# A gated linear attention and two dense layers on one core: the carried state is applied head by head on quarters of the array

## The chip, the core and the metric

The kernel runs on one core of a Trainium2 chip. TensorE (PE) multiplies matrices into PSUM; VectorE (DVE), ScalarE (ACT) and GpSimd (POOL) work element by element; DMA queues move data. The metric is the device time of one execution in microseconds (us); smaller is better. Nothing but float32 values enters or leaves.

## What is computed

For 4 batches of 8 heads, 768 steps and head size 48, each head keeps a 48x48 state that is decayed row by row with a gate and gets an outer product added at each step. The outputs of all heads are rows of 384 values, 3072 in all, which then pass through two dense layers with different activations.

```
f = 1 / (1 + exp(-f_logit))
for t in range(S):
    state = f[:, :, t, :, None] * state + einsum('bhd,bhe->bhde', k[:, :, t], v[:, :, t])
    y[:, :, t] = einsum('bhd,bhde->bhe', q[:, :, t], state)
h = max(x @ w_in, 0);  x = (h * h) @ w_out           # first layer, 384 -> 2048 -> 384
h = x @ w_in2;  g = h if h > 0 else exp(min(h, 0)) - 1;  out = g @ w_out2
```

## The kernel before

The 768 steps of each batch are cut into chunks of 128, so there are 24 chunks, numbered in order of time with the four batches taken in turn: chunk g belongs to batch g % 4. Two heads form a pair; there are four pairs, and their 2 x 48 channels lie on rows 0 to 47 and 64 to 111 (`HD`). A chunk passes through these steps:

- `a_gate`, `a_decay`: the gate, and its running products (two scans on VectorE).
- `a_scale`: queries and keys are multiplied with the products, on VectorE and GpSimd.
- `a_carry`: VectorE multiplies the batch's carried state with the decay of the chunk (line 186), and ScalarE copies it into `diag`, which holds a block-diagonal 112x112 matrix for each pair (line 188, two copies; the rest of `diag` was set to zero at the start).
- `a_scores`: keys are transposed (`tp`), and keys times queries make the scores of each head (`sc`, line 172), two heads at a time on the upper and the lower rows of the array. `a_mask` copies the scores under a mask into `ss`.
- `a_state`: keys times values (`kv`, line 201), which VectorE adds to the carried state in the same step (line 203).
- `a_out`: the outputs. For each pair and head, values times masked scores (line 229: 8 matmuls of all 128 rows, the two heads of a pair on the left and the right columns); then for each pair one matmul of `diag` with the queries on the whole array (line 234: 4 matmuls). ScalarE copies the results from PSUM into `x1` (lines 239 and 244), and six small DMAs distribute the fourth pair's rows.
- `a_hi`, `a_lo`: the outputs are split into a rounded part and a rest for the dense layers.

The first four chunks have no carried state and go by `a_direct`. The other 20 (chunks 4 to 23) have the matmuls of `diag`.

The dense layers work on six blocks of 512 rows each, and each block on 16 slices of 128 hidden features, so a layer has 96 units. A unit is `up` (9 matmuls into `ph`, line 343), `between` and `low` (the activation, on ScalarE, VectorE and GpSimd) and `down` (9 matmuls into `y`, line 395). Each of these 18 matmuls streams 512 columns. `down` runs two units behind `up`.

The order of the work is written out by hand: a plan gives each unit number ("slot") the steps that are issued ahead of that slot's `up`. Chunks 4 to 7 are finished during the first block (slots 0 to 15), and four further chunks during each of the next four blocks. During the first block the weights of the first layer are made as well, one slice per slot: a 64-bit word is decoded into float32 by ScalarE (line 46) and three VectorE instructions (lines 48, 51, 52), and is then split by ScalarE (`w`, line 312) and VectorE (`w`, line 313) into a rounded part and a rest. Unit f needs both. Each engine works strictly through its own list; within a slot the list has the chunk's steps first, then the load, decoding and splitting of weights.

Of the kernel before, what the change touches and what calls it, by code (L numbers as in the profile page):

```python
# [11 lines left out]
F32 = mybir.dt.float32  # L12
# [4 lines left out]
AF = mybir.ActivationFunctionType  # L17
ALU = mybir.AluOpType
PSUM = bass.MemoryType.PSUM

B, H, S, D = 4, 8, 768, 48
NT, DM, DFF = B * S, H * D, 2048
NG = NT // 128
NC = NG // B
NF = DFF // 128
NK = DM // 128
NP = H // 2
# [9 lines left out]
FIRST = (0, 3, 6, 8), (-6, -2, 2, 6)  # L37
STAGED = 15
DMIN = 2.0**-52


def decode(nc, raw, out):
# [12 lines left out]
def chunked(ctx, tc, ff, qk, vk, vz, wraw, mask, ident, flag, out):  # L55
# [23 lines left out]
    ds = [one.tile([ROWS, 2, 521], F32, name=f"ds{i}") for i in range(2)]  # L79
    ss = [one.tile([128, 2, NP, 128], F32, name=f"ss{i}") for i in range(2)]  # L80
    state = [one.tile([ROWS, NP, 48], F32, name=f"state{b}") for b in range(B)]
    diag = one.tile([ROWS, NP, ROWS], F32, name="diag")
    dlast = [one.tile([ROWS, NP], F32, name=f"dlast{b}") for b in range(B)]
    x2d = dram.tile([NK, 128, NT], F32, name="x2d")
    wst = dram.tile([NF, 128, 2, 2, DM], F32, name="wst")
# [97 lines left out]
    def a_carry(g):  # L183

        now = state[g % B]
        V.tensor_tensor(out=now, in0=now, in1=st[g]["wc"].unsqueeze(2).to_broadcast([ROWS, NP, 48]), op=ALU.mult)
        for lo, hi in HD:
            A.activation(diag[lo:hi, :, lo:hi], now[lo:hi], AF.Copy)

    def a_state(g):  # L190
        s = st[g]
        now = state[g % B]
        if g < NG - B:
            kvp = ps_a.tile([128, NP, 48], F32, tag="a", name=f"kv{g}")
            for p in range(NP):
                for j, (lo, hi) in enumerate(((0, 64), (64, ROWS))):
                    if g >= B:
                        v = s["vk"][:, p, j]
                    else:
                        v = s["vz"][:, p, j, 0:48] if p < NK else s["vz"][:, :, j, 96:112]  # L200
                    PE.matmul(kvp[lo:hi, p], s["kt"][:, p, lo:hi], v, start=True, stop=True)  # L201
            if g >= B:
                V.tensor_tensor(out=now, in0=kvp[:ROWS], in1=now, op=ALU.add)
            else:
                A.activation(now, kvp[:ROWS], AF.Copy)

    def a_direct(g):
        s = st[g]
        yp = ps_a.tile([128, NK, 128], F32, tag="a", name=f"yp{g}")
        for k in range(NK):  # L210
            for p, c in ((k, 0), (NK, 48)):
                for j in range(2):
                    PE.matmul(
                        yp[64 * j:64 * j + 64, k], s["vz"][:, k, j, c:c + 64], ss[g % 2][:, j, p],
                        start=c == 0, stop=c > 0,
                    )
        s["yp"] = yp

    def a_out(g):
        s = st[g]  # L220
        q = s["qk"][:, 0].rearrange("r (p t) -> r p t", p=NP)
        y3p = ps_a.tile([128, 128], F32, tag="a", name=f"y3p{g}")
        yp = ps_a.tile([128, NK, 128], F32, tag="a", name=f"yp{g}")

        outs = [(p, yp[:, p] if p < NK else y3p) for p in (NK, 0, 1, 2)]
        for p, o in outs:
            v = s["vk"][:, p].rearrange("r j d -> r (j d)")
            for j, c in enumerate((slice(0, 64), slice(48, 96))):
                PE.matmul(  # L229
                    o[64 * j:64 * j + c.stop - c.start], v[:, c], ss[g % 2][:, j, p],  # L230
                    start=p in (0, NK), stop=False, skip_group_check=True,
                )
        for p, o in outs:
            PE.matmul(o[:ROWS], diag[:, p], q[:, p], start=False, stop=p >= NK - 1, skip_group_check=True)  # L234
        x1 = two.tile([128, NK + 1, 128], F32, tag="x1", name=f"x1_{g}")
        y3, x1 = x1[:ROWS, NK], x1[:, :NK]

        for lo, hi in HD:
            A.activation(y3[lo:hi], y3p[lo:hi], AF.Copy)
        for k in range(NK):  # L240
            for lo, _ in HD:
                nc.sync.dma_start(out=x1[lo + 48:lo + 64, k], in_=y3[lo + 16 * k:lo + 16 * k + 16])
        for lo, hi in HD:
            A.activation(x1[lo:hi], yp[lo:hi], AF.Copy)
        s["x1"] = x1

    where = {}
# [168 lines left out]


    prepare = (a_gate,), (a_decay,), (a_scale, a_carry)
    finish = (a_scores, a_transposed, a_mask), (a_state, a_out), (), (), (a_hi, a_lo)
    for g in range(B, NG):  # L420
        i, o = where[g]
        d = o // 128
# [24 lines left out]
    with tc.manual_schedule():  # L447
        V.memset(lim, DMIN)
        V.memset(mn, 1.0)
        V.memset(ss[0], 0.0)  # L450
        G.memset(ss[1], 0.0)
        G.memset(diag, 0.0)

        warm = ps_a.tile([128, 512], F32, tag="a", name="warm")
        for _ in range(3):
            PE.matmul(warm, ss[0][:, 0, 0], ss[0][:, 0].rearrange("r p t -> r (p t)"), start=True, stop=True)
        steps = {
            "I": lambda: nc.sync.dma_start(out=idt, in_=ident),
            "M": lambda: nc.sync.dma_start(out=msk, in_=mask),
            "f": load_f, "q": load_qk, "v": load_v, "r": lambda f: load_raw(0, f),  # L460
            "g": a_gate, "d": a_decay, "c": a_scale, "s": a_scores, "t": a_transposed, "m": a_mask, "k": a_state,
            "y": a_direct, "h": a_hi, "l": a_lo,
            "w": lambda f: decode_weights(0, f), "W": lambda f: split_weights(0, f),
            "U": lambda f: up(0, f), "B": lambda f: between(0, f),
            "L": lambda f: low(0, f),
        }
        for o in START.split():
            steps[o[0]](*(int(c) for c in o[1:]))
        for u in range(2, len(units) + 2):

            last = units[u - 2] == (n1 - 1, NF - 1)
            todo = plan.get(u, ())
            for f, args in () if last else todo:
                f(*args)
            if u < len(units):
                up(*units[u])
            down(*units[u - 2])
            for f, args in todo if last else ():
                f(*args)
            if u < len(units):  # L480
                between(*units[u])
                low(*units[u])


def general(ctx, tc, nat, wraw, ident, out):
# [45 lines left out]
    with tc.For_i(0, 2, 1) as h, tc.For_i(0, B, 1) as b:  # L531
        y = yd[bass.ds(2 * b + h, 1)].rearrange("n p e j t -> (n p) e j t")
        for k in range(NK):
            for j in range(2):
                nc.sync.dma_start(out=x[64 * j:64 * j + 48, k], in_=y[k, :, j])
                nc.sync.dma_start(out=x[64 * j + 48:64 * j + 64, k], in_=y[NP - 1, 16 * k:16 * k + 16, j])
        for layer in range(2):
            V.memset(acc, 0.0)
            with tc.For_i(0, NF, 1) as ff:
# [43 lines left out]
def _layout(q, k, v, f_logit, moe_w_in, moe_w_out, moe2_w_in, moe2_w_out):  # L583
    fwd = np.arange(128)
    outward = np.r_[fwd[:64][::-1], fwd[64:]]

    def heads(a, order, pad):
        a = a.reshape(B, NP, 2, NC, 128, D)[:, :, :, :, order]
        t = np.full((NC, B, 2, 64, NP, 128), pad, a.dtype)
        t[:, :, :, :D] = a.transpose(3, 0, 2, 5, 1, 4)  # L590
        return t.reshape(NG, 128, 512)[:, :ROWS]


    ff = np.full((NG, ROWS, 521), -64.0, np.float32)
    ff[:, :, :520].reshape(NG, ROWS, 2 * NP, 65)[:, :, :, 1:] = heads(f_logit, outward, 8.0).reshape(NG, ROWS, 2 * NP, 64)
    qk = np.stack([heads(q, fwd, 0.0), heads(k, outward, 0.0)], axis=2)
    vk = v.reshape(B, NP, 2, NC, 128, D)[:, :, :, :, outward].transpose(3, 0, 4, 1, 2, 5).reshape(NG, 128, DM)
    vz = np.zeros((B, 128, NK, 2, 112), v.dtype)
    vp = vk[:B].reshape(B, 128, NP, 2, D)
    vz[..., :48] = vp[:, :, :NK]  # L600
    vz[..., 96:] = vp[:, :, NK].reshape(B, 128, 2, NK, 16).transpose(0, 1, 3, 2, 4)
    vz = vz.reshape(B, 128, -1)
    rows = []
    for kk in range(NK):
        for j in range(2):
            rows += [(2 * kk + j) * D + e for e in range(48)]
            rows += [(6 + j) * D + 16 * kk + e for e in range(16)]
    rows = np.array(rows)

    def weights(w_in, w_out):  # L610
        a = w_in.reshape(NK, 128, NF, 128).transpose(2, 1, 0, 3).reshape(NF, 128, DM)
        return np.concatenate([a, w_out.reshape(NF, 128, DM)], axis=2)

    wraw = np.stack([weights(moe_w_in[rows], moe_w_out), weights(moe2_w_in, moe2_w_out)]).view(np.int64)
    nat = np.zeros((B, NP, 4, 2, 64, S), np.float32)
    for c, a in enumerate((f_logit, q, k, v)):
        nat[:, :, c, :, :D] = a.reshape(B, NP, 2, S, D).transpose(0, 1, 2, 4, 3)
    nat = nat.reshape(B, NP, 4, 128, S)[:, :, :, :ROWS]
    mask = (outward[:, None] <= fwd[None, :]).astype(np.int32)
    return {  # L620
        "ff": ff, "qk": qk, "vk": vk, "vz": vz, "nat": nat, "wraw": wraw, "mask": mask,
        "ident": np.eye(128, dtype=np.float32),
    }
# [13 lines left out]
```

## Time and profile before

| | |
|---|---|
| median of 3 runs | 944.69 us (943.04 to 944.89) |
| profiled execution, its own time | 943.66 us |
| its span, first to last instruction | 941.9 us |
| mean granted TensorE clock | 0.981 of full speed |
| busy: TensorE matmuls / VectorE / ScalarE / GpSimd | 913.2 / 564.4 / 455.8 / 327.1 us |

The rows further down are from this one execution. A float32 matmul of an attention step leaves two records in the trace, one for each part of its weights; a matmul of the dense layers leaves one. Records of a row marked xN follow each other or overlap: the row's first number is the start of its first record, the second the time from there to the end of its last. A record's end is modelled and lies past the start of the next, so the pace of a stream is read from starts. A number in brackets is the idle time of the engine ahead of the row, with what ended it.

### The profile page before, as it was taken

What the parts mean: (1) busy time and instruction counts of PE and PEld (TensorE: products, weight loads), DVE (VectorE), ACT (ScalarE), POOL (GpSimd) and SP (SyncE); (2) the same over time, 40 slices, a digit from 0 to 9 for tenths busy, and PEclk for the clock granted to TensorE, in tenths of its full rate; (3) what the DMA queues carried; (4) which work ended last, traced back from release to release, by engine and by line L of the source; (5) the groups of instructions that cost most, each with busy time, mean ns of one, the idle gap of its engine ahead of it and who ended that gap; (6) DMA issues with size and microseconds to landing.
All of it is one profiled execution on the core that took longest, in us unless ns stands there. A gap on an engine that the chain in (4) does not pass through costs nothing.

```text
span 941.9 us, 13099 instructions
## 1 busy us (share of the span) xinstructions
PE 913.2 (97%) x4841; PEld 740.8 (79%) x4841; DVE 564.4 (60%) x834; ACT 455.8 (48%) x791; POOL 327.1 (35%) x295
## 2 busy tenths in 40 slices
PE   6888989999999999999999999999999999999996
PEld 4766768888888888788888888888888888888885
DVE  8888886667667766775401166456555555555543
ACT  4457664554445445454444444444444444443543
POOL 5222323443444443444233232332332333233231
PEclk8799899999999999999999999999999999999998
DMA  8445423444433443442246530100100100100001
GB/s 277 141 141 192 131 67 123 135 137 141 141 108 109 143 142 126 154 146 78 94 158 213 174 135 1 57 12 1 56 12 1 56 13 0 57 12 1 34 0 37
DMA packets 30791, 88.44 MB, mean 94 GB/s; under 512 B 4992, under 2 KB 9728, under 8 KB 30720
## 3 DMA queue, kind: packets, MB, share of 16 engines
q1 hardware_dynamic: 28848, 77.32, 24.7%
q10 hardware_dynamic: 1872, 10.22, 3.2%
q8 instruction: 39, 0.64, 0.3%
q14 instruction: 32, 0.26, 0.1%
HBM read 64.52 MB, written 22.02 MB: 92 GB/s over the span
## 4 chain that ended last, share of the span: by engine, by line
PE 87%; DVE 8%; issue 2%; ACT 1%; DMA 1%; POOL 0%; ACTq 0%; DVEq 0%
PE y L395 40%; PE ph L343 40%; PE sc L172 2%; DVE dec L51 1%; DVE w L313 1%; PE yp L229 1%; PE yp L234 1%; DVE ds L136 1%; DVE dec L52 1%; PE kv L201 1%; DVE dec L48 1%; PE y3p L234 1%; DVE ss L181 1%; PE tp L166 1%; PE y3p L229 1%
## 5 line engine op out<-in xcount | busy, mean ns | idle before, releaser
L382 POOL TENSOR_TENSOR gl<-gg,gh 128x512 fp32r<-128x512 f32 x175 | 232.5, 1328 | 489.6 <-PE ph L343 193.5
L395 PE MATMUL y<-gh,w 128*128 128x512 f32 x576 | 179.9, 393 | 0.0
L395 PE MATMUL y<-gh,wf 128*128 128x512 f32 (+1 forms) x582 | 179.6, 390 | 0.0
L343 PE MATMUL ph<-xh,w 128*128 128x512 f32 x576 | 158.6, 410 | 11.2 <-ACT w L312 7.5
L368 DVE SCALAR_TENSOR_TENSOR t<-r,t 128x512 f32<-128x512 f32 (+1 forms) x97 | 71.5, 737 | 162.4 <-ACT r L367 161.3
L343 PE MATMUL ph<-xh,wf 128*128 128x512 f32 (+1 forms) x582 | 147.8, 389 | 0.0
L364 ACT ACTIVATE r<-ph 128x512 f32<-128x512 f32 (+1 forms) x97 | 57.6, 594 | 186.0 <-PE ph L343 176.7
L343 PEld LDWEIGHTS ph<-xh,w 128*128 128x128 f32 x576 | 107.1, 192 | 38.5 <-ACT w L312 9.2
L395 PEld LDWEIGHTS y<-gh,w 128*128 128x128 f32 x576 | 108.9, 189 | 24.9
L395 PEld LDWEIGHTS y<-gh,wf 128*128 128x128 f32 x582 | 108.9, 188 | 24.4 <-ACT gh L371 0.2
L343 PEld LDWEIGHTS ph<-xh,wf 128*128 128x128 f32 x582 | 108.6, 188 | 23.7
L395 PE MATMUL y<-gl,wf 128*128 128x512 f32 (+1 forms) x291 | 112.8, 388 | 0.0
L395 PE MATMUL y<-gl,w 128*128 128x512 f32 x288 | 112.5, 391 | 0.0
L356 ACT ACTIVATE r<-ph 128x512 f32<-128x512 f32 x96 | 56.9, 593 | 91.1 <-PE ph L343 73.5
L343 PE MATMUL ph<-xl,w 128*128 128x512 f32 x288 | 84.7, 403 | 0.2 <-DVE xl L269 0.2
L343 PE MATMUL ph<-xl,wf 128*128 128x512 f32 (+1 forms) x291 | 82.2, 391 | 0.0
L362 DVE TENSOR_TENSOR gh<-r 128x512 fp32r<-128x512 f32 x64 | 44.5, 696 | 48.6 <-ACT r L356 48.1
L369 DVE SCALAR_TENSOR_TENSOR gg<-ph,t 128x512 f32<-128x512 f32 (+1 forms) x97 | 66.6, 686 | 10.0
L343 PEld LDWEIGHTS ph<-xl,w 128*128 128x128 f32 x288 | 56.1, 195 | 13.2 <-DVE xl L269 0.6
L357 ACT ACTIVATE gg<-r 128x512 f32<-128x512 f32 x96 | 60.8, 633 | 8.0 <-ACT r L356 0.4
L395 PEld LDWEIGHTS y<-gl,wf 128*128 128x128 f32 x291 | 54.7, 188 | 12.1 <-DVE gl L376 0.2
L395 PEld LDWEIGHTS y<-gl,w 128*128 128x128 f32 x288 | 54.2, 188 | 12.4
(84 smaller groups left out, 1067.3 us busy)
## 6 DMA issues: line engine op xcount, KB each, us to landing
raw<-wraw SPq DMA_DIRECT2D x19, 768.0 KB, 4.5
wst<-w SPq DMA_DIRECT2D x16, 768.0 KB, 4.0
wf<-wst SPq DMA_DIRECT2D x16, 768.0 KB, 4.3
qk<-qk SPq DMA_DIRECT2D x24, 448.0 KB, 5.4
raw<-wraw ACTq DMA_DIRECT2D x13, 768.0 KB, 4.4
ff<-ff SPq DMA_DIRECT2D x22, 227.9 KB, 4.5
x2d<-yo SPq DMA_DIRECT2D x18, 256.0 KB, 2.3
x<-x2d SPq DMA_DIRECT2D x18, 256.0 KB, 3.1
```

Source lines behind the costliest of these rows:

```text
L172: PE.matmul(sc[j][:, p], k[lo:hi, p], q[lo:hi, p], start=True, stop=True)
L229: PE.matmul(o[64 * j:64 * j + c.stop - c.start], v[:, c], ss[g % 2][:, j, p], start=p in (0, NK), stop=False, skip_group_check=True,)
L234: PE.matmul(o[:ROWS], diag[:, p], q[:, p], start=False, stop=p >= NK - 1, skip_group_check=True)
L343: PE.matmul(ph, w[:, a, 0, 128 * k:128 * k + 128], b[:, k, c], start=(m == 0), stop=(m == len(todo) - 1))
L356: A.activation(r[:, c], ph, AF.Relu)
L357: A.activation(gg[:, c], r[:, c], AF.Square)
L362: V.tensor_tensor(out=gh[:, c], in0=r[:, c], in1=r[:, c], op=ALU.mult)
L364: A.activation(r[:, c], ph, AF.Relu, scale=-1.0)
L368: V.scalar_tensor_tensor(out=t[:, c], in0=r[:, c], scalar=1.0, in1=t[:, c], op0=ALU.add, op1=ALU.mult)
L369: V.scalar_tensor_tensor(out=gg[:, c], in0=ph, scalar=0.0, in1=t[:, c], op0=ALU.max, op1=ALU.add)
L382: G.tensor_tensor(out=gl, in0=gg, in1=gh, op=ALU.subtract)
L395: PE.matmul(yp_[i][m][:, c], w[:, a, 1, 128 * m:128 * m + 128], b[:, c], start=(f == 0 and n_ == 0), stop=(f == NF - 1 and n_ == 2 and c.s ...
```

## The change

The block-diagonal matrices are gone, with their two ScalarE copies per chunk and their clearing at the start. In `a_out` the carried state of each head is now the weight of a matmul of its own, 48 rows by 48 columns, with the same head's rows of the queries: 8 matmuls in place of 4. The input rows of a head (0 or 64) are fixed; its output rows are 0 or 64, and for pairs 2 and 3 the two heads are swapped (`at_`), so that four heads of two pairs use the four quarters of the array. Pairs 0 and 1 go to one PSUM tile, pairs 2 and 3 to another; four copies of 48x256 take them to `x1` in place of two of 48x128 and two of 48x384, the fourth pair's tile first. The values' matmuls (8, all 128 rows) are now all 48 columns wide. Because the state is read by `a_out` now, the addition of `kv` to it becomes a step of its own, `a_add`, one slot later. The host's tables are permuted in the same manner (the values of the first four chunks, the rows of the first weight matrix).

```
+def at_(p, j):
+    return j if p < 2 else 1 - j
...
-        for lo, hi in HD:
-            A.activation(diag[lo:hi, :, lo:hi], now[lo:hi], AF.Copy)
...
-                V.tensor_tensor(out=now, in0=kvp[:ROWS], in1=now, op=ALU.add)
+                s["kv"] = kvp
...
+    def a_add(g):
+        if g < NG - B:
+            now = state[g % B]
+            V.tensor_tensor(out=now, in0=st[g]["kv"][:ROWS], in1=now, op=ALU.add)
...
-        y3p = ps_a.tile([128, 128], F32, tag="a", name=f"y3p{g}")
-        yp = ps_a.tile([128, NK, 128], F32, tag="a", name=f"yp{g}")
-        outs = [(p, yp[:, p] if p < NK else y3p) for p in (NK, 0, 1, 2)]
-        for p, o in outs:
-            v = s["vk"][:, p].rearrange("r j d -> r (j d)")
-            for j, c in enumerate((slice(0, 64), slice(48, 96))):
+        o = [ps_a.tile([128, 2, 128], F32, tag="a", name=f"o{g}_{i}") for i in range(2)]
+        for p in (0, 2, 1, 3):
+            for j in range(2):
+                r = 64 * at_(p, j)
                 PE.matmul(
-                    o[64 * j:64 * j + c.stop - c.start], v[:, c], ss[g % 2][:, j, p],
-                    start=p in (0, NK), stop=False, skip_group_check=True,
+                    o[p // 2][r:r + 48, p % 2], s["vk"][:, p, j], ss[g % 2][:, j, p],
+                    start=p % 2 == 0, stop=False, skip_group_check=True,
                 )
-        for p, o in outs:
-            PE.matmul(o[:ROWS], diag[:, p], q[:, p], start=False, stop=p >= NK - 1, skip_group_check=True)
+        for p in (0, 2, 1, 3):
+            for j, (lo, hi) in enumerate(HD):
+                r = 64 * at_(p, j)
+                PE.matmul(
+                    o[p // 2][r:r + 48, p % 2], state[g % B][lo:hi, p], q[lo:hi, p],
+                    start=False, stop=p % 2 == 1, skip_group_check=True,
+                )
...
-        for lo, hi in HD:
-            A.activation(y3[lo:hi], y3p[lo:hi], AF.Copy)
-        for lo, hi in HD:
-            A.activation(x1[lo:hi], yp[lo:hi], AF.Copy)
+        for i in (1, 0):
+            for lo, hi in HD:
+                A.activation(x1[lo:hi, 2 * i:2 * i + 2], o[i][lo:hi], AF.Copy)
...
-    finish = (a_scores, a_transposed, a_mask), (a_state, a_out), (), (), (a_hi, a_lo)
+    finish = (a_scores, a_transposed, a_mask), (a_state, a_out), (a_add,), (), (a_hi, a_lo)
...
-        G.memset(diag, 0.0)
```

On TensorE, the outputs of chunk 8 stand like this before; `y3p8` and `yp8` are the PSUM tiles of the fourth and of the first three pairs, `vk8` the values, `qk8` the queries.

```order
L229 MATMUL y3p8_1288<-ss0_89,vk8_1066 64x128
L229 MATMUL y3p8_1288<-ss0_89,vk8_1066 48x128
L229 MATMUL yp8_1289<-ss0_89,vk8_1066 64x128
L229 MATMUL yp8_1289<-ss0_89,vk8_1066 48x128
L229 MATMUL yp8_1289<-ss0_89,vk8_1066 64x128
L229 MATMUL yp8_1289<-ss0_89,vk8_1066 48x128
L229 MATMUL yp8_1289<-ss0_89,vk8_1066 64x128
L229 MATMUL yp8_1289<-ss0_89,vk8_1066 48x128
L234 MATMUL y3p8_1288<-qk8_917,diag_95 112x128
L234 MATMUL yp8_1289<-qk8_917,diag_95 112x128 x3
```

On TensorE, the same place of the changed kernel; `o8_0` is the tile of pairs 0 and 1, `o8_1` that of pairs 2 and 3, `state0` the carried state.

```order
L235 MATMUL o8_0_1291<-ss0_89,vk8_1068 48x128 x2
L235 MATMUL o8_1_1292<-ss0_89,vk8_1068 48x128 x2
L235 MATMUL o8_0_1291<-ss0_89,vk8_1068 48x128 x2
L235 MATMUL o8_1_1292<-ss0_89,vk8_1068 48x128 x2
L242 MATMUL o8_0_1291<-qk8_917,state0_91 48x128 x2
L242 MATMUL o8_1_1292<-qk8_917,state0_91 48x128 x2
L242 MATMUL o8_0_1291<-qk8_917,state0_91 48x128 x2
L242 MATMUL o8_1_1292<-qk8_917,state0_91 48x128 x2
```

The four matmuls of 112 rows of output became eight of 48, alternating in twos between the tiles; the eight ahead of them keep their number.

On ScalarE, this stood in slot 10 of the first block before: the copies of chunk 6's outputs, the two copies into `diag` for chunk 7, chunk 8's gate, and the rounded part of weight slice 11.

```order
L239 ACTIVATE x1_6_982<-y3p6_968 48x128 x2
L244 ACTIVATE x1_6_982<-yp6_969 48x384 x2
L188 ACTIVATE diag_95<-state3_94 48x4x48 x2
L125 ACTIVATE ff8_915<-ff8_915 112x521
L312 ACTIVATE w0_11_1002<-dec0_11_922 128x768
L46 ACTIVATE dec0_12_1005<-raw0_12_927 128x768
```

On ScalarE, the same place of the changed kernel.

```order
L249 ACTIVATE x1_6_985<-o6_1_968 48x256 x2
L249 ACTIVATE x1_6_985<-o6_0_967 48x256 x2
L129 ACTIVATE ff8_915<-ff8_915 112x521
L323 ACTIVATE w0_11_1003<-dec0_11_922 128x768
L51 ACTIVATE dec0_12_1006<-raw0_12_927 128x768
```

Between the outputs' copies and weight slice 11 nothing is left that reads the carried state.

On VectorE, slots 10 and 11 of the first block before: `state2` is the addition for chunk 6, `state3` the decay for chunk 7, `w0_11` the rest of weight slice 11.

```order
L376 TENSOR_TENSOR gl0_9_949<-gg0_9_951,gh0_9_948 128x512
L271 TENSOR_TENSOR xl1_751<-x1_5_778,xh1_750 128x3x128
L203 TENSOR_TENSOR state2_93<-kv6_958,state2_93 112x192
L157 TENSOR_TENSOR qk7_801<-qk7_801,ds1_88 112x4x64
L158 TENSOR_TENSOR qk7_801<-qk7_801,ds1_88 112x4x64
L186 TENSOR_TENSOR state3_94<-state3_94,wc7_910 112x192
L313 TENSOR_TENSOR w0_11_1002<-dec0_11_922,w0_11_1002 128x768
```

On VectorE, the same place of the changed kernel, up to the masked copy of chunk 7's scores.

```order
L387 TENSOR_TENSOR gl0_9_949<-gg0_9_951,gh0_9_948 128x512
L282 TENSOR_TENSOR xl1_749<-x1_5_779,xh1_748 128x3x128
L161 TENSOR_TENSOR qk7_802<-qk7_802,ds1_88 112x4x64
L162 TENSOR_TENSOR qk7_802<-qk7_802,ds1_88 112x4x64
L190 TENSOR_TENSOR state3_94<-state3_94,wc7_910 112x192
L324 TENSOR_TENSOR w0_11_1003<-dec0_11_922,w0_11_1003 128x768
L53 TENSOR_SCALAR dec0_12_1006<-dec0_12_1006 128x768
L56 SCALAR_TENSOR_TENSOR dec0_12_1006<-raw0_12_927,dec0_12_1006 128x768
L57 SCALAR_TENSOR_TENSOR dec0_12_1006<-raw0_12_927,dec0_12_1006 128x768
L387 TENSOR_TENSOR gl0_10_1033<-gg0_10_1035,gh0_10_1032 128x512
L212 TENSOR_TENSOR state2_93<-kv6_958,state2_93 112x192
L185 COPY_PREDICATED ss1_90<-msk_83,sc7_0_1046 128x512
```

The addition moved from ahead of the scaling of chunk 7's queries to behind slice 12's decoding; everything else on VectorE keeps its order.

## Rows read from the trace of the kernel before

**Rows 1.** The page: busy time of TensorE, and its granted clock in 40 slices.

```profile
PE 913.2 (97%) x4841; PEld 740.8 (79%) x4841; DVE 564.4 (60%) x834; ACT 455.8 (48%) x791; POOL 327.1 (35%) x295
PEclk8799899999999999999999999999999999999998
```

**Rows 2.** Busy time by stretch: length, engines with their instructions, granted clock, DMA.

```profile
35.00:125.60 90.60, 77.87 (x457) 59.70 (x457) 79.23 (x120) 56.54 (x100) 27.74 (x25) 0.91 0.45 147
125.60:455.00 329.40, 329.39 (x2033) 268.29 (x2034) 225.91 (x322) 167.35 (x310) 135.21 (x132) 1.00 0.39 127
```

**Rows 3.** Waits from 35 to 125.6 us: us in total, times, longest.

```profile
ACT diag L188 <- DVE state L186: 23.4, 5, 6.2
...
DVE w L313 <- ACT w L312: 9.7, 6, 2.2
...
PE ph L343 <- ACT w L312: 7.5, 6, 2.3
...
PE ph L343 <- DVE w L313: 2.0, 4, 0.5
```

**Rows 4.** VectorE in order of time, 103 to 109.5 us (slot 10).

```profile
103.04 1.33 DVE L52 SCALAR_TENSOR_TENSOR dec<-raw,dec 128x768 uint32<-128x768 uint32 x1
...
104.30 0.68 DVE L376 TENSOR_TENSOR gl<-gg,gh 128x512 fp32r<-128x512 f32 x1
...
105.37 0.34 DVE L203 TENSOR_TENSOR state<-kv,state 112x192 f32<-112x192 f32 x1
...
106.31 0.34 DVE L186 TENSOR_TENSOR state<-state,wc 112x192 f32<-112x192 f32 x1
108.84 0.96 DVE L313 TENSOR_TENSOR w<-dec,w 128x768 fp32r<-128x768 f32 x1 [2.19 <-ACT w L312]
```

**Rows 5.** ScalarE in order of time, the same stretch.

```profile
101.43 0.98 ACT L244 ACTIVATE x<-yp 48x384 f32<-48x384 f32 x2
106.68 0.36 ACT L188 ACTIVATE diag<-state 48x192 f32<-48x192 f32 x1 [4.27 <-DVE state L186]
...
107.99 0.83 ACT L312 ACTIVATE w<-dec 128x768 fp32r<-128x768 f32 x1
```

**Rows 6.** VectorE in order of time: the first and the last of its six waits.

```profile
41.45 0.96 DVE L313 TENSOR_TENSOR w<-dec,w 128x768 fp32r<-128x768 f32 x1 [0.31 <-ACT w L312]
...
124.60 0.96 DVE L313 TENSOR_TENSOR w<-dec,w 128x768 fp32r<-128x768 f32 x1 [1.65 <-ACT w L312]
```

**Rows 7.** TensorE in order of time, behind one of these waits.

```profile
108.86 0.50 PE L343 MATMUL ph<-xh,w 128*128 128x512 f32 x1 [1.18 <-ACT w L312]
109.86 2.13 PE L343 MATMUL ph<-xh,w 128*128 128x512 f32 x5 [0.49 <-DVE w L313]
```

**Rows 8.** TensorE in order of time: the outputs of one chunk, 156 to 160.4 us.

```profile
156.32 0.61 PE L201 MATMUL kv<-vk,kt 128*64 128x48 f32 x15
156.72 0.30 PE L229 MATMUL y3p<-ss,vk 128*48 128x128 f32 x1
156.77 0.22 PE L201 MATMUL kv<-vk,kt 128*64 128x48 f32 x1
...
156.97 0.91 PE L229 MATMUL yp<-ss,vk 128*48 128x128 f32 x12
157.81 0.47 PE L234 MATMUL y3p<-qk,diag 112*112 112x128 f32 x2
158.12 0.82 PE L234 MATMUL yp<-qk,diag 112*112 112x128 f32 x6
158.69 1.64 PE L343 MATMUL ph<-xh,w 128*128 128x512 f32 x6
```

**Rows 9.** TensorE in order of time: a plain unit's start, and scores followed by one.

```profile
142.18 1.52 PE L343 MATMUL ph<-xh,w 128*128 128x512 f32 x6
...
150.91 1.16 PE L172 MATMUL sc<-qk 48*128 48x128 f32 x16
152.00 1.63 PE L343 MATMUL ph<-xh,w 128*128 128x512 f32 x6
```

More of the change, by code (lines that the diff above doesn't have):

```diff
@@ L81, in chunked @@
     state = [one.tile([ROWS, NP, 48], F32, name=f"state{b}") for b in range(B)]
-    diag = one.tile([ROWS, NP, ROWS], F32, name="diag")
     dlast = [one.tile([ROWS, NP], F32, name=f"dlast{b}") for b in range(B)]
@@ L199, in a_state @@
                     else:
-                        v = s["vz"][:, p, j, 0:48] if p < NK else s["vz"][:, :, j, 96:112]
+                        v = s["vz"][:, p, at_(p, j), 0:48] if p < NK else s["vz"][:, :, at_(p, j), 96:112]
                     PE.matmul(kvp[lo:hi, p], s["kt"][:, p, lo:hi], v, start=True, stop=True)
             if g >= B:
-                V.tensor_tensor(out=now, in0=kvp[:ROWS], in1=now, op=ALU.add)
+                s["kv"] = kvp
             else:
                 A.activation(now, kvp[:ROWS], AF.Copy)
+    def a_add(g):
+        if g < NG - B:
+            now = state[g % B]
+            V.tensor_tensor(out=now, in0=st[g]["kv"][:ROWS], in1=now, op=ALU.add)
     def a_direct(g):
@@ L213, in a_direct @@
                     PE.matmul(
-                        yp[64 * j:64 * j + 64, k], s["vz"][:, k, j, c:c + 64], ss[g % 2][:, j, p],
+                        yp[64 * j:64 * j + 64, k], s["vz"][:, k, j, c:c + 64], ss[g % 2][:, at_(p, j), p],
                         start=c == 0, stop=c > 0,
@@ L221, in a_out @@
         q = s["qk"][:, 0].rearrange("r (p t) -> r p t", p=NP)
-        y3p = ps_a.tile([128, 128], F32, tag="a", name=f"y3p{g}")
-        yp = ps_a.tile([128, NK, 128], F32, tag="a", name=f"yp{g}")
-        outs = [(p, yp[:, p] if p < NK else y3p) for p in (NK, 0, 1, 2)]
-        for p, o in outs:
-            v = s["vk"][:, p].rearrange("r j d -> r (j d)")
-            for j, c in enumerate((slice(0, 64), slice(48, 96))):
+        o = [ps_a.tile([128, 2, 128], F32, tag="a", name=f"o{g}_{i}") for i in range(2)]
+        for p in (0, 2, 1, 3):
+            for j in range(2):
+                r = 64 * at_(p, j)
                 PE.matmul(
-                    o[64 * j:64 * j + c.stop - c.start], v[:, c], ss[g % 2][:, j, p],
-                    start=p in (0, NK), stop=False, skip_group_check=True,
-                )
-        for p, o in outs:
-            PE.matmul(o[:ROWS], diag[:, p], q[:, p], start=False, stop=p >= NK - 1, skip_group_check=True)
-        x1 = two.tile([128, NK + 1, 128], F32, tag="x1", name=f"x1_{g}")
-        y3, x1 = x1[:ROWS, NK], x1[:, :NK]
-        for lo, hi in HD:
-            A.activation(y3[lo:hi], y3p[lo:hi], AF.Copy)
-        for k in range(NK):
-            for lo, _ in HD:
-                nc.sync.dma_start(out=x1[lo + 48:lo + 64, k], in_=y3[lo + 16 * k:lo + 16 * k + 16])
-        for lo, hi in HD:
-            A.activation(x1[lo:hi], yp[lo:hi], AF.Copy)
+                    o[p // 2][r:r + 48, p % 2], s["vk"][:, p, j], ss[g % 2][:, j, p],
+                    start=p % 2 == 0, stop=False, skip_group_check=True,
+                )
+        for p in (0, 2, 1, 3):
[5 more added lines that the diff above has]
+                )
+        x1 = two.tile([128, NK + 1, 128], F32, tag="x1", name=f"x1_{g}")
+        for i in (1, 0):
+            for lo, hi in HD:
+                A.activation(x1[lo:hi, 2 * i:2 * i + 2], o[i][lo:hi], AF.Copy)
+            if i:
+                for k in range(NK):
+                    for lo, _ in HD:
+                        nc.sync.dma_start(out=x1[lo + 48:lo + 64, k], in_=x1[lo + 16 * k:lo + 16 * k + 16, NK])
+        x1 = x1[:, :NK]
         s["x1"] = x1
@@ L534, in general @@
             for j in range(2):
-                nc.sync.dma_start(out=x[64 * j:64 * j + 48, k], in_=y[k, :, j])
-                nc.sync.dma_start(out=x[64 * j + 48:64 * j + 64, k], in_=y[NP - 1, 16 * k:16 * k + 16, j])
+                nc.sync.dma_start(out=x[64 * j:64 * j + 48, k], in_=y[k, :, at_(k, j)])
+                nc.sync.dma_start(
+                    out=x[64 * j + 48:64 * j + 64, k], in_=y[NP - 1, 16 * k:16 * k + 16, at_(NP - 1, j)]
+                )
         for layer in range(2):
@@ L599, in _layout @@
     vp = vk[:B].reshape(B, 128, NP, 2, D)
-    vz[..., :48] = vp[:, :, :NK]
-    vz[..., 96:] = vp[:, :, NK].reshape(B, 128, 2, NK, 16).transpose(0, 1, 3, 2, 4)
+    for kk in range(NK):
+        for j in range(2):
+            vz[:, :, kk, j, :48] = vp[:, :, kk, at_(kk, j)]
+            vz[:, :, kk, j, 96:] = vp[:, :, NK, at_(NK, j), 16 * kk:16 * kk + 16]
     vz = vz.reshape(B, 128, -1)
@@ L605, in _layout @@
         for j in range(2):
-            rows += [(2 * kk + j) * D + e for e in range(48)]
-            rows += [(6 + j) * D + 16 * kk + e for e in range(16)]
+            rows += [(2 * kk + at_(kk, j)) * D + e for e in range(48)]
+            rows += [(2 * NK + at_(NK, j)) * D + 16 * kk + e for e in range(16)]
     rows = np.array(rows)
```

## The prediction

> **What bounds the kernel now.** I read the page first: TensorE is busy for 97% of the span, and its granted clock is below full speed in the first slices only [rows 1]. The busy times by stretch say where the other 3% lie [rows 2]: from 125.6 to 455 us TensorE is busy for 329.39 of 329.40 us at clock 1.00, while from 35 to 125.6 us, which is most of the first block, it is busy for 77.87 of 90.60 us at clock 0.91. So the change has to be judged in two places by two measures. Chunks 8 to 23 (16 of the 20 that used `diag`) issue their outputs behind 125.6 us: there a chunk's time on TensorE is time of the kernel. Chunks 4 to 7 fall into the stretch where TensorE waits.
>
> What it waits for there is the next reading. The waits of that stretch [rows 3] give 7.5 us for `w` of ScalarE and 2.0 us for `w` of VectorE, the two parts of a weight slice. One step back, VectorE itself waits six times, 9.7 us in total, and always for `w` of ScalarE; it is busy for 79.23 of the 90.60 us [rows 2], the rest being gaps of some hundredths between instructions. One step further, ScalarE waits 23.4 us in five places, and always in `diag` for the decayed state of VectorE. In order of time it is a loop through two lists. In slot 10 [rows 4, 5] VectorE ends the decoding of slice 11 at about 104.4, and ScalarE, idle since about 102.4, could split it at once; but its list has the `diag` copies first, which need the state that VectorE decays at 106.31. They start at 106.68; only at 107.99 does ScalarE split the slice (0.83), and VectorE, idle for 2.19 us, takes the rest at 108.84. TensorE idles 1.18 and 0.49 us behind that, and its next five matmuls take 2.13 us where a plain row of six takes 1.52 [rows 7, 9]: the clock is at the lower of its two levels (1.2 of 2.4 GHz) for a while. Of VectorE's six waits, the first is 0.31 us and has no copy ahead of it, the last is 1.65 us [rows 6]; the five with a copy sum to 9.7 - 0.31 = 9.4 us.
>
> **The change, part by part.**
>
> *Removing the copies (first block).* With `diag` gone, ScalarE's list goes from the outputs' copies to the gate and to `w`. In slot 10 it can run `w` from 104.4 to 105.2. What is late next is VectorE alone: between the end of decoding and the rest of the slice its list has `gl`, the scaling of the queries and the decay, up to 106.6 [rows 4], which covers ScalarE's 0.83 us. So the five waits go, and as VectorE has no other wait in the stretch, everything behind each moves up by its length: 9.4 us at most. TensorE can follow: its 77.87 busy us contain slowed stretches, and even so they leave 12.7 us idle. Behind 125.6 us slices 14 and 15 follow with the distances of before, so the gain is kept when TensorE becomes the bound. What can eat of it: the raw weights' DMA, which is queued behind `diag` too and starts earlier with it; TensorE being late with scores for the masks; and one new wait. That is chunk 7's scores: with `kv` held a slot longer, their second PSUM tile is the one that ScalarE must first empty of `tp`. I take 9.0 us, the sum less about one state addition (0.34). The bounds are 9.4 and 0: nothing, if another wait closes each gap.
>
> *The state's matmuls (chunks 8 to 23).* Before: eight records of `diag`, from 157.81 [rows 8]. The ends of the two rows (158.28 and 158.94) lie six records apart, so one takes 0.11; the first two starts lie 0.31 before the row of six, so 0.09 of the first weight load is not covered. The last is through at 158.12 + 6 x 0.11 = 158.78. The following `ph` row ends 1.55 behind that, 0.03 more than plain [rows 9]: no price, since both use the whole array. In all 0.97 + 0.03 = 1.00 us.
>
> After: 16 records of 48 columns in four quarters. The trace has no quarters. It has two column halves, 16 records of values in two streams, and two row halves, the scores. In both, two streams run side by side at one record's pace each: `yp`'s twelve records take 0.91 us where one stream at 0.11 would need 1.3 [rows 8], the scores' sixteen 1.16 where it would need 1.76 [rows 9]. If four run like that, four records follow each other in each quarter: 4 x 0.11 = 0.44. To this come the uncovered load, between 0 and 0.09, of which I take half (48 columns for 112), and the return to the whole array. The scores show that: they are through at about 150.91 + 1.16 - 0.16 = 151.91 (0.16 is the modelled tail, 0.82 - 6 x 0.11), and the `ph` row behind ends 1.72 later in place of 1.52, so 0.20. Sum 0.44 + 0.05 + 0.20 = 0.69: a chunk gains 0.3 us, 16 chunks 4.8. Bounds for a chunk: 0.36 better with the load covered; if only two streams run, 0.88 in place of 0.44, which is 0.14 worse; if one, 1.76, which is 1.02 worse.
>
> A row speaks on whether streams wait for each other: a record of `y3p` on the 48-column half starts at 156.72, ahead of `kv`'s last on the 64-column half at 156.77 [rows 8], though it stands behind it in the list. The Trainium skill says otherwise (TensorE: Matmul & The Clock Gate, "The mechanism"): matmuls start strictly in their order. By that rule the two records of each head would hold up the next head, nine steps or 0.99 us, 0.25 worse per chunk; the trace disagrees, and the sum goes by the trace.
>
> *The rest.* The addition moves by a slot and stays one instruction; it no longer makes VectorE wait for `kv`. In the first block it leaves the list ahead of slice 11 and joins it later: nothing. The four copies have as many elements as before. The six small DMAs are issued behind the state's last matmul, some 0.2 us later in the unit; their reader stands three slots on. The clearing of `diag` was at the start on GpSimd. All this lies beside other work: 0.
>
> *Sum.* Against the profiled execution, 943.66 - 9.0 - 4.8 = 929.9 us. It lies 1.03 under the median of the runs, so against these 944.69 - 13.8 = 930.9; I say 931.
>
> **Rivals.**
>
> *Two quarters at a time.* Both halves of a pair write the same PSUM tile from different rows of the array. The rows show two column halves in one tile (`yp`) and two row halves in two tiles (`sc`), but nowhere two row halves in one. If the hardware lets only one row half write a tile at a time, a chunk is 0.14 worse: 944.69 - 9.0 + 2.2 = 938. The Trainium skill states such a rule (TensorEngine Tiling (Array Packing), "Gotcha 1: PSUM Pressure"): different row tiles cannot access the same PSUM bank simultaneously. No run here shows it; against it stands that the two heads use different partitions.
>
> *The gaps of the first block are closed by something else.* TensorE, slowed behind each remaining wait, could bring scores or `ph` too late, or raw weights could land too late. For it: the lower clock in this stretch. Against it: TensorE's 12.7 us of idle time. With none of the 9.0, 944.69 - 4.8 = 940; with half, 935.
>
> *Slower: the quarters run one by one.* Then a chunk costs 1.02 us more, 16.3 in all, 944.69 - 9.0 + 16.3 = 952. It decides from 0.56 us per chunk on (9.0 / 16). For it: no row shows quarters. Against it: both kinds of halves run side by side.
>
> **How the numbers follow.** The forecast 0.72, its own range 928 to 934 (down: 9.4 and 16 x 0.36 make 929.5, and the fastest run lies 1.65 under the median; up: two thirds of the 9.0 and the 4.8 make 934). Two at a time 0.12; gaps closed otherwise 0.10; one by one 0.04; the remaining 0.02 for no change. The range 928 to 939 holds the first two and the half-way form of the third. What this measurement can tell from no change is about 0.2%, 1.9 us: faster 0.94 (the first three), same 0.02, slower 0.04.
>
> **What would show it.** Right: no wait of VectorE for `w` from 35 us to the end of the first block's weights, and the rest of the slice that now starts at 124.60 [rows 6] some 9 us earlier; between a chunk's values and the next `ph`, 16 records of the state whose starts come in fours, and about 0.7 us in place of 1.0. Wrong: starts in twos with 1.1 us or more; VectorE waiting for scores or `gh` in the first block; a wait of TensorE behind 125.6 us.

## The result, and the profile after

The changed kernel takes 929.83 us (median of 4 runs, 927.88 to 930.30) against 943.87 us of the kernel before, timed beside it on the same chip (median of 4, 942.65 to 944.89). The ratio is 0.9844, with an interval of 0.9827 to 0.9861: 1.6% faster, and the forecast of 931 is 1.2 us off. The profiled execution took 927.88 us, its span is 926.1 us.

The page of the kernel after, its busy times and the granted clock (before: [rows 1]):

```profile
PE 897.8 (97%) x5001; PEld 724.5 (78%) x5001; DVE 564.7 (61%) x834; ACT 441.5 (48%) x751; POOL 359.6 (39%) x294
PEclk8999999999999999999999999999999999999999
```

TensorE runs 160 records more (20 chunks, 16 for 8) and yet is busy for 15.4 us less; ScalarE has 40 copies fewer. The clock is at nine tenths or more in every slice but the first. The same two stretches as in [rows 2], busy time by stretch; the first ends earlier now, since the first block does:

```profile
35.00:116.00 81.00, 70.68 (x488) 54.49 (x488) 78.92 (x117) 53.32 (x91) 28.51 (x25) 0.96 0.50 163
116.00:445.00 329.00, 329.00 (x2183) 263.97 (x2182) 226.13 (x324) 156.03 (x279) 167.53 (x132) 1.00 0.38 128
```

VectorE is busy for 78.92 of 81.00 us of the first stretch, so it sets its pace alone. TensorE is busy for all of the second. The waits of the first stretch (total, times, longest) answer to [rows 3]:

```profile
ACT w L323 <- DVE dec L57: 17.9, 9, 5.3
...
PE ph L354 <- DVE w L324: 4.2, 3, 2.0
...
PE ph L354 <- ACT w L323: 1.6, 1, 1.6
...
PE sc L176 <- ACT kt L181: 1.2, 1, 1.2
...
DVE w L324 <- ACT w L323: 0.3, 1, 0.3
```

The wait of VectorE for ScalarE's part of the slice fell from 9.7 us in six places to 0.3 us in one, the one that had no copy ahead of it. ScalarE still waits, but now in `w` itself, for VectorE's decoding, which `w` needs. Slot 10 in order of time, VectorE (before: [rows 4]):

```profile
95.86 1.33 DVE L57 SCALAR_TENSOR_TENSOR dec<-raw,dec 128x768 uint32<-128x768 uint32 x1
97.11 1.10 DVE L387 TENSOR_TENSOR gl<-gg,gh 128x512 fp32r<-128x512 f32 x1
...
99.27 0.35 DVE L190 TENSOR_TENSOR state<-state,wc 112x192 f32<-112x192 f32 x1
99.54 0.95 DVE L324 TENSOR_TENSOR w<-dec,w 128x768 fp32r<-128x768 f32 x1
```

and ScalarE (before: [rows 5]):

```profile
93.98 0.64 ACT L129 ACTIVATE ff<-ff 112x521 f32<-112x521 f32 x1
97.22 0.85 ACT L323 ACTIVATE w<-dec 128x768 fp32r<-128x768 f32 x1 [2.60 <-DVE dec L57]
```

`gl` is longer than it was (1.10 for 0.68), of which more below. ScalarE splits the slice at 97.22, as soon as the decoding is through, and is done at 98.07. VectorE comes to the rest of the slice at 99.54 straight from the decay, without the 2.19 us of idle time that stood there. One chunk's outputs on TensorE (before: [rows 8]):

```profile
145.00 0.61 PE L203 MATMUL kv<-vk,kt 128*64 128x48 f32 x15
...
145.50 1.04 PE L235 MATMUL o<-ss,vk 128*48 128x128 f32 x15
146.47 0.65 PE L242 MATMUL o<-qk,state 48*48 48x128 f32 x16
147.05 1.66 PE L354 MATMUL ph<-xh,w 128*128 128x512 f32 x6
```

What the state costs here can be read from such rows in one way for all kernels: from its first start to the end of the `ph` row behind it, less the 1.52 us of a plain row [rows 9]. Before, that is 158.69 + 1.64 - 157.81 - 1.52 = 1.00 us [rows 8]; after, 147.05 + 1.66 - 146.47 - 1.52 = 0.72 us. A window of 0.14 us at the start of that row, cut out of the same list, shows how many of the sixteen have started by then:

```profile
146.47 0.33 PE L242 MATMUL o<-qk,state 48*48 48x128 f32 x4
```

Four started within 0.02 us. The next four follow 0.15 us later, and then four each 0.11 us.

**Where the 15.8 us went.** Three marks split the profiled executions: VectorE's start on the rest of slice 2 (in the kernel before it is the first line of [rows 6]), on the rest of slice 13 (its last line), and the span's end. In the kernel after the two starts are

```profile
39.10 0.96 DVE L324 TENSOR_TENSOR w<-dec,w 128x768 fp32r<-128x768 f32 x1 [0.31 <-ACT w L323]
...
113.55 0.95 DVE L324 TENSOR_TENSOR w<-dec,w 128x768 fp32r<-128x768 f32 x1
```

The same for all kernels, in us; the last column is TensorE's granted clock from 20 to 31 us:

| kernel | start to slice 2 | slice 2 to 13 | slice 13 to end | clock 20 to 31 |
|---|---|---|---|---|
| before | 41.45 | 83.15 | 817.3 | 0.57 |
| after | 39.10 | 74.45 | 812.55 | 1.00 |
| e1, copies a slot later | 41.29 | 74.28 | 817.5 | 0.54 |
| e2, copies kept | 41.32 | 83.97 | 813.1 | 0.61 |
| e3, two quarters | 38.93 | 74.46 | 819.7 | 1.00 |
| e4, pairs in order | 41.46 | 74.38 | 813.1 | 0.61 |
| e5, addition in its old slot | 38.97 | 74.75 | 812.5 | 1.00 |
| e6, a subtraction on GpSimd | 41.58 | 75.14 | 813.1 | 0.50 |

Before to after: 8.70 us in the first block (forecast 9.0), 4.75 behind it (forecast 4.8), and 2.35 ahead of it, which was not forecast. That e2 and e6 take 813.1 us behind slice 13 and after 812.55 is not TensorE's: to the end of its last matmul it is 809.8 us before, 805.0 after, and 805.0 in e2 and e6 as well. The difference lies behind it, in the last DMA. The 2.35 us do not come with the change each time: e4 and e6, which are the changed kernel but for an edit far behind the start, start like the kernel before. They go with the clock of the early stretch. From 20 to 31 us, busy time by stretch, of before, of after and of e4:

```profile
20.00:31.00 11.00, 9.10 (x89) 8.27 (x90) 8.19 (x12) 2.90 (x6) 5.58 (x7) 0.57 0.42 138
```

```profile
20.00:31.00 11.00, 7.58 (x137) 7.07 (x139) 10.65 (x15) 4.88 (x9) 5.66 (x7) 1.00 0.47 159
```

```profile
20.00:31.00 11.00, 9.68 (x102) 8.58 (x99) 8.38 (x13) 3.51 (x7) 5.82 (x7) 0.61 0.42 138
```

Near the lower of its two levels (1.2 and 2.4 GHz) TensorE gets through 89 or 102 records in these 11 us in place of 137, and VectorE behind it through 12 or 13 instructions in place of 15. Call a start with the clock at 1.00 there a quick one. The times differ by as much: 927.88 (the profiled execution, with a quick start) and 930.3 among those of after. Whether the change makes a quick start more frequent is not shown: three of the five profiles without `diag` have one, and none of the three with it (before, e1, e2), though e1's fastest run, 2.1 us under its others, may be one. So a difference of 2 us between two single runs says nothing here. A kernel should be judged by the marks or by like starts.

### The profile page after: what moved, and what is told of

The parts are those of the page before. It is cut to its first block, busy times and chain, and to the rows that moved or that the text cites. A ratio compares the mean times of both kernels' runs of the same rounds, so it can differ in the third digit from the quotient of the medians.

```text
span 926.1 us, 13344 instructions
## 1 busy us (share of the span) xinstructions
PE 897.8 (97%) x5001; PEld 724.5 (78%) x5001; DVE 564.7 (61%) x834; ACT 441.5 (48%) x751; POOL 359.6 (39%) x294
## 4 chain that ended last, share of the span: by engine, by line
PE 89%; DVE 7%; issue 1%; ACT 1%; POOL 1%; DMA 0%; DVEq 0%; ACTq 0%
PE ph L354 42%; PE y L406 41%; PE sc L176 2%; PE o L235 2%; DVE dec L56 1%; PE o L242 1%; DVE ds L140 1%; DVE dec L57 1%; DVE w L324 1%; PE kv L203 1%; DVE dec L53 1%; DVE ss L185 1%; DVE gl L387 1%; PE tp L170 0%; DVE ds L142 0%
## 5 line engine op out<-in xcount | busy, mean ns | idle before, releaser
L393 POOL TENSOR_TENSOR gl<-gg,gh 128x512 fp32r<-128x512 f32 x175 | 245.8, 1405 | 470.5 <-PE ph L354 199.3
L354 PE MATMUL ph<-xh,w 128*128 128x512 f32 x576 | 154.5, 403 | 6.9 <-DVE w L324 4.2
L354 PEld LDWEIGHTS ph<-xh,w 128*128 128x128 f32 x576 | 105.0, 188 | 35.9 <-DVE w L324 5.4
```

What stands on the lines that cost most here:

```text
L354: PE.matmul(ph, w[:, a, 0, 128 * k:128 * k + 128], b[:, k, c], start=(m == 0), stop=(m == len(todo) - 1))
L393: G.tensor_tensor(out=gl, in0=gg, in1=gh, op=ALU.subtract)
```

## The experiments

The change does two things: no copies into `diag`, and quarters in place of block-diagonal matmuls. e1 and e2 separate them (e1 moves the copies, e2 has the quarters and keeps the copies), e3 and e4 ask how the quarters run, e5 asks about the moved addition, e6 tries to gain more. None leaves out part of the computation; e2 makes copies that nothing reads. The kernel before had a median of 944.37 us beside e1 to e4 and of 943.60 beside e5 and e6.

**e1: the kernel before, its two copies one slot later.**

```diff
     def a_carry(g):
         ...
         V.tensor_tensor(out=now, in0=now, ..., op=ALU.mult)
+
+    def a_diag(g):
+        now = state[g % B]
         for lo, hi in HD:
             A.activation(diag[lo:hi, :, lo:hi], now[lo:hi], AF.Copy)
...
-    finish = (a_scores, a_transposed, a_mask), (a_state, a_out), (), (), (a_hi, a_lo)
+    finish = (a_diag, a_scores, a_transposed, a_mask), (a_state, a_out), (), (), (a_hi, a_lo)
```

> The kernel before, with the two ScalarE copies into the block-diagonal tile issued one slot later, ahead of the chunk's scores, so that they no longer stand ahead of a weight slice; the matmuls of the block-diagonal state stay. Theory (two separate gains: 8.7 to 9.4 us because the copies no longer hold ScalarE back in the first block, 4.5 to 4.8 us from the quarters): 944 - 9 = 935 us, VectorE's waits for the slice's rounded part fall from 9.7 to about 0.3 us, and the state's matmuls stay at 1.0 us a chunk. Rival (most of the gain is TensorE's in all 20 chunks, the first block only follows): 941 to 944 us. Rival (it is the removal of the copies' 14.5 us of ScalarE work, not their place): 941 to 944 us as well, with the waits still there.

Measured: 934.9 us (932.72 to 935.19), ratio 0.9896 (0.9879 to 0.9914). The first block takes 74.28 us, as after; behind it the kernel takes 817.5 us, as before. VectorE's two marks, waits of e1 from 35 to 116 us, and ScalarE in order of time:

```profile
41.29 0.96 DVE L316 TENSOR_TENSOR w<-dec,w 128x768 fp32r<-128x768 f32 x1 [0.31 <-ACT w L315]
...
115.57 0.94 DVE L316 TENSOR_TENSOR w<-dec,w 128x768 fp32r<-128x768 f32 x1
```

```profile
DVE w L316 <- ACT w L315: 0.3, 1, 0.3
```

```profile
98.98 0.85 ACT L315 ACTIVATE w<-dec 128x768 fp32r<-128x768 f32 x1 [2.64 <-DVE dec L52]
...
102.34 0.72 ACT L191 ACTIVATE diag<-state 48x192 f32<-48x192 f32 x2
```

The copies are all there, but behind `w` in ScalarE's list, and the five waits are gone. It was the place of the copies, not their work, that cost the first block its time.

**e2: the kernel after, with the copies where they were.**

```diff
+    diag = one.tile([ROWS, NP, ROWS], F32, name="diag")
...
     def a_carry(g):
         ...
+        for lo, hi in HD:
+            A.activation(diag[lo:hi, :, lo:hi], now[lo:hi], AF.Copy)
...
+        G.memset(diag, 0.0)
```

> The changed kernel, with the block-diagonal tile, its clearing at the start and the two copies per chunk put back at their old place; nothing reads the tile. Theory: the gain of the first block goes and the one of the quarters stays: 929.8 + 9 = 939 us, with VectorE again waiting about 9 us for ScalarE in the first block. Rival (TensorE's shorter chunk alone brings the gain): 930 to 931 us.

Measured: 938.87 us (938.1 to 940.23), ratio 0.9943 (0.9926 to 0.9959). The mirror image of e1: 83.97 us in the first block, 813.1 behind it. Its waits from 35 to 126 us are those of [rows 3] again, and VectorE in order of time has the two marks and one wait that is new:

```profile
ACT diag L193 <- DVE state L191: 20.3, 4, 6.3
DVE w L327 <- ACT w L326: 10.2, 6, 2.2
```

```profile
41.32 0.96 DVE L327 TENSOR_TENSOR w<-dec,w 128x768 fp32r<-128x768 f32 x1 [0.31 <-ACT w L326]
...
113.22 1.34 DVE L186 COPY_PREDICATED ss<-msk,sc 128x512 f32<-128x512 int32 x2 [0.46 <-PE sc L177]
...
125.29 0.96 DVE L327 TENSOR_TENSOR w<-dec,w 128x768 fp32r<-128x768 f32 x1 [2.18 <-ACT w L326]
```

Nothing reads these copies. They only take ScalarE's time and their place in its list, and that costs 83.97 - 74.45 = 9.5 us; e1, with the same copies elsewhere, says that it is the place. e2 is 0.8 us longer than the kernel before between the marks: its last wait is 2.18 us in place of 1.65 [rows 6], and VectorE waits 0.46 us for chunk 7's scores.

**e3: the same 16 records, on two quarters.** With `at_` returning `j`, no pair is swapped: every head's output rows follow its input rows (0 to 0, 64 to 64), so that only two of the four quarters are used.

```diff
-    return j if p < 2 else 1 - j
+    return j
```

> The changed kernel without the swap of heads for pairs 2 and 3, so that a head's output rows follow its input rows and only two of the four quarters are used. Theory (each quarter takes one stream at 0.11 us a record): the state's 16 records take 0.88 us in place of 0.44, from 0.7 to 1.14 us a chunk in all; 16 chunks behind the first block cost 7.0 us more, 929.8 + 7.0 = 937 us; the first block stays, as VectorE sets it. Rival (the pace is set by weight loads or by the queue, not by the number of quarters): 930 us.

Measured: 934.86 us (934.83 to 937.71), ratio 0.9913 (0.9893 to 0.9933). The two expectations lie 7 us apart, and the marks carry the verdict: 819.7 us behind the first block, 7.15 more than after and 2.4 more than before. The expected 937 is met between like starts (937.71 against 930.3, or 934.83 against 927.88); by their times, most of its runs had a quick start. The views are VectorE's second mark, one chunk on TensorE in order of time, and the state's row cut off about 0.14 us behind its start:

```profile
113.39 0.94 DVE L324 TENSOR_TENSOR w<-dec,w 128x768 fp32r<-128x768 f32 x1
```

```profile
145.70 1.04 PE L235 MATMUL o<-ss,vk 128*48 128x128 f32 x15
146.67 1.08 PE L242 MATMUL o<-qk,state 48*48 48x128 f32 x16
147.67 1.66 PE L354 MATMUL ph<-xh,w 128*128 128x512 f32 x6
```

```profile
146.67 0.31 PE L242 MATMUL o<-qk,state 48*48 48x128 f32 x2
```

The starts come in twos, and the state costs 147.67 + 1.66 - 146.67 - 1.52 = 1.14 us. So what pays behind the first block is that four quarters run. The same records on two of them are slower than the old block-diagonal ones.

**e4: the pairs in the order 0, 1, 2, 3.** Pairs 0 and 1 use the same two quarters, so the list now has eight records for two quarters ahead of the first one for the other two.

```diff
-        for p in (0, 2, 1, 3):
+        for p in (0, 1, 2, 3):
```

> The changed kernel with the state's matmuls in the order of pairs 0, 1, 2, 3 in place of 0, 2, 1, 3, so that the list has eight records for one pair of quarters before the first for the other pair. Theory (a quarter starts its next record as soon as it is free, wherever it stands in TensorE's queue): no change, 930 us, starts still in fours. Rival (TensorE looks only a few records ahead): starts in twos, 0.88 us in place of 0.44, 937 us; part of it, 931 to 936.

Measured: 930.62 us (928.49 to 931.0), ratio 0.9852 (0.9834 to 0.9869): as after. TensorE, the same two views of e4:

```profile
148.75 0.67 PE L242 MATMUL o<-qk,state 48*48 48x128 f32 x16
149.35 1.66 PE L354 MATMUL ph<-xh,w 128*128 128x512 f32 x6
```

```profile
148.75 0.34 PE L242 MATMUL o<-qk,state 48*48 48x128 f32 x4
```

Four still start together, and the state costs 0.74 us. The rows do not name the pairs, so what follows is worked out: in e3 two quarters start no more than two records at a time, so of the first four here two are of the other two quarters, and they start while six or more records that stand before them in the list have not.

**e5: the addition of `kv` back in the slot of the outputs.**

```diff
-    finish = ..., (a_state, a_out), (a_add,), (), (a_hi, a_lo)
+    finish = ..., (a_state, a_out, a_add), (), (), (a_hi, a_lo)
```

> The changed kernel with the addition of the keys-times-values product put back into the slot of the chunk's outputs, behind them. Theory (the place of the addition costs and brings nothing: VectorE is behind TensorE in the first block and has room later): 930 us, the stretch from weight slice 2 to slice 13 on VectorE still 74.4 us; behind the first block VectorE waits for the state's matmuls, up to 2.5 us a chunk, without a wait of TensorE. Rival (the later slot is what kept VectorE's list free): VectorE waits in the first block too, up to 1.6 us at each of four chunks, 932 to 936 us.

Measured: 928.32 us (927.94 to 929.91), ratio 0.9845 (0.9828 to 0.9862): no difference from after. Over the whole span VectorE waits 12 times for it:

```profile
DVE state L212 <- PE o L242: 30.9, 12, 2.8
```

None of these waits lies between the two marks of the first block (74.75 us). Behind it they are paid from VectorE's idle time, as TensorE is the bound there (812.5 us). So moving the addition was neutral, as forecast.

**e6: can VectorE's list in the first block be made shorter?** The subtraction that forms `xl` goes to GpSimd for the first chunks.

```diff
-            V.tensor_tensor(out=lo, in0=st.pop(g)["x1"], in1=hi, op=ALU.subtract)
+            (G if g < 2 * B else V).tensor_tensor(out=lo, in0=st.pop(g)["x1"], in1=hi, op=ALU.subtract)
```

> The changed kernel with the rest of the split outputs (a subtraction of 128x384) of chunks 4 to 7 on GpSimd in place of VectorE. Theory (VectorE alone sets the first block now): two subtractions of 0.47 us leave VectorE's list between weight slices 2 and 13, that stretch goes from 74.4 to 73.5 us, 929 us in all. Rival (GpSimd's work slows VectorE's decoding beside it, whose instructions of 0.96 us take 1.33 beside GpSimd's scaling): 74.4 us or more, 930 us or more.

Measured: 930.25 us (928.27 to 931.62), ratio 0.9853 (0.9831 to 0.9876); the stretch takes 75.14 us, 0.7 more than after in place of less. VectorE of e6 in order of time, and GpSimd at that moment:

```profile
75.19 0.96 DVE L56 SCALAR_TENSOR_TENSOR dec<-raw,dec 128x768 uint32<-128x768 uint32 x1
76.18 1.66 DVE L57 SCALAR_TENSOR_TENSOR dec<-raw,dec 128x768 uint32<-128x768 uint32 x1
```

```profile
75.39 1.64 POOL L282 TENSOR_TENSOR xl<-x,xh 128x384 fp32r<-128x384 f32 x1 [3.35 <-DMA raw<-wraw]
```

The decoding at 75.19 is under way when GpSimd's subtraction begins and takes 0.96 us, though most of it runs beside the subtraction; the next one begins with the subtraction under way and takes 1.66. At the second subtraction it is `mn`, 0.15 us long elsewhere, that is held up; VectorE and GpSimd:

```profile
95.68 1.05 DVE L145 TENSOR_TENSOR mn<-mn,ds 112x8 f32<-112x8 f32 x1
```

```profile
95.71 0.99 POOL L282 TENSOR_TENSOR xl<-x,xh 128x384 fp32r<-128x384 f32 x1
```

So VectorE's list gave up two subtractions of 0.47 us, 0.94, and lost 0.70 + 0.90 = 1.60 us in these two places: 0.66 of the 0.69 us. The rival was right, and from slice 2 to the end no kernel tried here beats the changed one.

## Why the prediction was right

**The copies (9.0 forecast, 8.70 measured).** The loop read from [rows 3] to [rows 5] was the cause: e1 takes the wait out by place alone, e2 puts it back by place alone. Between the two marks VectorE's waits for `w` fall by 9.4 us, all that the forecast counted. The allowance taken off them, 0.4, was named wrongly: it was put at about one more state addition, while in fact one addition fewer stands between the marks. What ate 1.3 us was `gl`. That 9.0 lies so near to 8.70 is in part luck: the forecast had neither of these two terms. Groups of VectorE's instructions between the marks, before and after (busy time, mean ns | idle time before them):

```profile
L376 DVE TENSOR_TENSOR gl<-gg,gh 128x512 fp32r<-128x512 f32 x11 | 7.5, 682 | 0.0
...
L203 DVE TENSOR_TENSOR state<-kv,state 112x192 f32<-112x192 f32 x4 | 1.4, 348 | 0.0
```

```profile
L387 DVE TENSOR_TENSOR gl<-gg,gh 128x512 fp32r<-128x512 f32 x11 | 8.8, 798 | 0.0
...
L212 DVE TENSOR_TENSOR state<-kv,state 112x192 f32<-112x192 f32 x3 | 1.0, 348 | 0.0
```

So 9.4 + 0.35 - 1.3 = 8.45 of the 8.70 are in two groups; the rest is in hundredths of the others. The longer `gl` comes from the new timing. GpSimd in order of time, slot 10 of before and of after:

```profile
108.17 0.63 POOL L129 TENSOR_SCALAR ff<-ff 112x521 f32<-112x521 f32 x1 [4.61 <-ACT ff L125]
```

```profile
96.34 1.34 POOL L133 TENSOR_SCALAR ff<-ff 112x521 f32<-112x521 f32 x1
```

Before, GpSimd's `ff` ran while VectorE sat in its wait (until 108.84, [rows 4]) and took 0.63 us. After, it begins at 96.34, under VectorE's decoding (95.86 to 97.19), takes 1.34 us and ends 0.49 us behind the decoding. `gl` begins at 97.11, while `ff` is under way, takes 1.10 us and ends 0.53 behind `ff`. So each is longer by its wait for the one before it; three of the eleven `gl` are that long. The wait that was removed had covered it. This was read from the rows and not tried by itself; e6 has the like.

TensorE kept up: it is idle for 10.3 us of the 81, and its mean clock there rose from 0.91 [rows 2] to 0.96, with fewer waits.

**The new wait came, and cost nothing.** TensorE in order of time shows chunk 7's scores held up by ScalarE's copy of `tp`, as was said:

```profile
99.50 0.46 PE L176 MATMUL sc<-qk 48*128 48x128 f32 x2 [0.89 <-ACT r L367]
101.16 1.16 PE L176 MATMUL sc<-qk 48*128 48x128 f32 x14 [1.21 <-ACT kt L181]
102.25 2.55 PE L354 MATMUL ph<-xh,w 128*128 128x512 f32 x6
```

The 1.21 us and the slowed `ph` row behind them (2.55 for 1.52) fall on an engine that has idle time in this stretch, and VectorE shows no wait for scores there. It was not free in itself: in e2, which keeps the copies, the same wait is 4.9 us long, and VectorE waits 0.46 us behind it.

**The quarters (0.69 forecast against 1.00, 0.72 measured).** Streams on parts of the array run side by side at one record's pace each. That was worked out from two halves, and held for four. 16 x 0.28 = 4.5 by the rows, 4.75 by the marks; the rest lies ahead of the state, where `kv`'s first start and the state's are 1.49 us apart before [rows 8] and 1.47 after. The rival's price held too: two quarters were put at 0.14 us worse than before for a chunk (its terms, 0.88 + 0.05 + 0.20, make 0.13), and e3 is 1.14 - 1.00 = 0.14 worse.

**The rule of row halves in one tile.** In the quarters two row halves write the same tile on different partitions: pairs 0 and 1 use two of the quarters and one tile, pairs 2 and 3 the others. After shows four starts within 0.02 us, so both halves write each tile at once, and 0.72 us for 16 records. With one half at a time only two streams would run, which costs the 1.14 us of e3. The Trainium skill (TensorEngine Tiling (Array Packing), "Gotcha 1: PSUM Pressure") has row tiles unable to access one PSUM bank simultaneously; by that rule the time would have been 938, and the traces do not agree with it for halves that write different partitions.

**The rule of strict order.** In the list of the changed kernel a head's second record stands ahead of the next head's first, and still four records start within 0.02 us, where two quarters start two (e3). e4 lists eight records of two quarters ahead of the others, and four start together there too. The Trainium skill (TensorE: Matmul & The Clock Gate, "The mechanism") has matmuls start strictly in their order; the traces do not agree with it for matmuls on different parts of the array, here as in [rows 8]. So the sentence that each engine works strictly through its own list fits VectorE and ScalarE in these rows, but not TensorE's starts on different parts of the array.

**The rest.** The addition moved for nothing (e5). The other rivals fell: the gaps of the first block were not closed by something else, and the quarters did not run one by one. What the prediction did not have is the start: the profile that it was summed against begins near the lower clock (0.57 from 20 to 31 us), and the forecast of 931 was met within 1.2 us by a median over runs that differ by 2.4, which is in part chance. By the marks, like with like, it was 0.35 us too high on a gain of 13.8.

## What to carry to other kernels

Follow a chain of waits through every in-order list that it crosses: here a copy that nobody was waiting for stood ahead of one that everybody was waiting for, and moving it by a slot (e1) was worth 9 us without doing less work. Here small matmuls paid on quarters of the array only with all four in use; count the streams before the records. Where runs differ at their start, set marks in the trace and compare stretch by stretch: the two profiled executions by themselves would have given this change 2.35 us that e4 and e6, which have the change too, do not show.

## What the runs showed of the hardware that was not expected

- TensorE's granted clock from 20 to 31 us differs between executions: 1.00 in three of the profiles, 0.50 to 0.61 in the other five, and on both sides among the changed kernel and e3 to e6, which have the same steps there. It goes with about 2.4 us at the mark of slice 2. What decides it stays open; no run tried to set it.
- Four quarters of 48x48 run at once at one record's pace each (0.11 us for 128 columns), with row halves that share a tile, and in e4 a record for a free part starts past six or more that stand before it in the list.
- VectorE and GpSimd hold each other up: a decoding of 128x768 that is under way when GpSimd's subtraction begins takes 0.96 us, the next one, begun beside it, 1.66; `ff` on GpSimd takes 1.34 us in place of 0.63 when it begins under a decoding. So handing work to GpSimd gained nothing (e6).
